# Ones column in v, PSUM scratch for half A's conversion, thresholds on ScalarE, reordered first loads, turns in half B

## The chip, the cores and the metric

One core of one Trainium2 chip. The metric is the device time of one execution in microseconds (us), lower is better.

## What is computed

Attention with a threshold on 4 batches of 8 heads, 576 positions of 64 numbers, and behind it two dense layers with gates on 2304 tokens (512 to 2048 to 512 each). All data are float32.

```python
scores = scale * np.matmul(q, k.transpose(0, 1, 3, 2))
thresh = np.max(scores, axis=-1, keepdims=True) - tau
scores = np.where(scores >= thresh, scores, -1000000000.0)
attn = np.exp(scores - np.max(scores, axis=-1, keepdims=True))
attn = attn / (np.sum(attn, axis=-1, keepdims=True) + 1e-09)
x = heads_to_columns(np.matmul(attn, v))          # [2304, 512]
h = x @ w1_in;  x = (h * np.clip(h + 3, 0, 6) / 6) @ w1_out
h = x @ w2_in;  return (h - np.tanh(h)) @ w2_out
```

## The kernel before

Every product is made from operands that are split in a high and a low part, three matmuls for one (`mm3`), so most tensors exist twice. The weights come as float32 and are converted on the chip.

**Who orders the work.** The kernel records tasks with `add(engine, duration, key, ...)`, and `Plan.issue` (L90) lays them out when the program is built: it plays the engines forward in time with the given durations, and whenever an engine is free it issues the task with the smallest key among those whose inputs are ready. The order on each engine is fixed by that; on the chip each engine goes through its list in order and waits at semaphores. A key is a priority and no time. Rings of buffers (`Ring`) are part of it; rings with `free=True` choose their slot when the task is issued. `slack` holds back a task's successors, and a buffer's reuse, in the plan only.

**Attention.** A unit (`softmax`, L556) is one head and 128 queries, or the last 64 queries of two heads (`c == NC`); there are 144. TensorE makes the scores into one of two PSUM buffers `s` (L580), VectorE takes the negative maximum (L585), ScalarE the exponential (L587), VectorE computes the threshold from the maximum (L589, one column) and multiplies the exponentials by "score at least threshold" (L592), where an accumulator gives the sum of the weights. ScalarE rounds the result to 16 bits (L597), GpSimd subtracts for the low part (L601), a transposing DMA on the queue of SP turns it (L604), and TensorE multiplies it with v (L637, `weighted`), from where ScalarE copies it into `x` (L647). The sums get 1e-9 added, are multiplied with v's scale (L609) and inverted (L613, L618) on VectorE. `v_round` (L505) scales and splits v, `k_round` and `q_round` transpose and split k and q. `x_round` (L655) normalises a block of x on GpSimd (L670), transposes and splits it. LK, LQ, LV tell how many units ahead k, q and v are prepared.

**First layer, half A.** The hidden dimension of 2048 is cut in halves of 8 pieces of 128. Half A runs beside attention, in 8 groups of 256 or 320 tokens (`layer1`, L700), as soon as a group's x is there. It accumulates in two PSUM banks of the ring `R_m`. Its 16 weights (`load_w`, L330) are converted beside the first units: a load on SP's queue, ScalarE's absolute value into the SBUF scratch `wu` (L353), four steps on VectorE on 512 columns (L356, L358, L361, L364), ScalarE's copy (L370) and GpSimd's subtraction (L372).

**First layer, half B, and second layer.** After attention the memory of attention is freed and taken for a second set of weights ("b"; the first is "a"). Half B goes through 9 blocks of 256 tokens: for each of 8 pieces `hidden` (12 matmuls, gate) and a second product (12 matmuls) into four PSUM banks, of which a block takes two. The blocks come one after the other. Its in weights are converted into the buffers "a", its out weights into "b". The second layer has its blocks 0 and 1 taking turns by halves already; its weights of the first half go to "b" (in) and "a" (out), those of the second to "a" (in) and "b" (out).

## Time and profile before

| | |
|---|---|
| median of 3 runs | 1166.88 us (1164.44 to 1168.1) |
| profiled execution | 1166.68 us |
| its span, first to last instruction | 1164.8 us |
| TensorE busy, mean granted clock | 1074.1 us, 0.959 |
| VectorE busy | 743.8 us |
| ScalarE busy | 608.8 us |
| GpSimd busy | 426.7 us |

PE is TensorE, PEld its loading of weights, DVE is VectorE, ACT is ScalarE, POOL is GpSimd, SP only issues DMAs. Times of an engine are the union of its instructions in time. Instructions that follow each other on one engine can overlap a little. A granted clock of 1 is TensorE's full speed.

### The profile page before, as it was taken

What the parts mean: (1) busy time and instruction counts of PE and PEld (TensorE: products, weight loads), DVE (VectorE), ACT (ScalarE), POOL (GpSimd) and SP (SyncE); (2) the same over time, 40 slices, a digit from 0 to 9 for tenths busy, and PEclk for the clock granted to TensorE, in tenths of its full rate; (3) what the DMA queues carried; (4) which work ended last, traced back from release to release, by engine and by line L of the source; (5) the groups of instructions that cost most, each with busy time, mean ns of one, the idle gap of its engine ahead of it and who ended that gap; (6) DMA issues with size and microseconds to landing.
All of it is one profiled execution on the core that took longest, in us unless ns stands there. A gap on an engine that the chain in (4) does not pass through costs nothing.

```text
span 1164.8 us, 23412 instructions
## 1 busy us (share of the span) xinstructions
PE 1074.1 (92%) x9104; PEld 1001.5 (86%) x9104; DVE 743.8 (64%) x1651; ACT 608.8 (52%) x1214; POOL 426.7 (37%) x412
## 2 busy tenths in 40 slices
PE   5647699999999899889899999999999999999998
PEld 4546689998999799888799999977999999999997
DVE  6999978688878877667766664697333333333332
ACT  7656678688768876554444443454323323233222
POOL 3665767666756675562321120265200000000000
PEclk8567899999999999999899999999999999999999
DMA  7788677869977767788543332132000000000000
GB/s 198 161 171 184 132 151 178 185 136 197 159 168 148 166 128 152 167 225 271 173 130 91 91 93 55 55 115 67 19 19 19 1 19 19 1 19 18 1 19 19
DMA packets 257455, 125.79 MB, mean 108 GB/s; under 512 B 200256, under 2 KB 250944, under 8 KB 257344
## 3 DMA queue, kind: packets, MB, share of 16 engines
q1 hardware_dynamic: 247840, 114.85, 42.3%
q0 software_dynamic: 9504, 9.44, 3.5%
q8 instruction: 72, 1.18, 0.4%
q14 instruction: 39, 0.32, 0.1%
HBM read 62.92 MB, written 18.87 MB: 70 GB/s over the span
## 4 chain that ended last, share of the span: by engine, by line
PE 46%; POOL 2%; issue 2%; DVE 1%; ACT 0%; POOLq 0%; DVEq 0%; ACTq 0%
PE ya L382 23%; PE h L382 12%; PE m L382 11%; POOL g L697 1%; POOL bo L372 1%; DVE st L361 0%; POOL ai L372 0%; DVE st L364 0%; DVE wu L358 0%; DVE y L925 0%; ACT x L938 0%; DVE wu L356 0%; DVE wu L991 0%; DVE x L941 0%; ACT ai L370 0%
## 5 line engine op out<-in xcount | busy, mean ns | idle before, releaser
L601 POOL TENSOR_TENSOR pp<-e,pp 128x128 f16<-128x128 f32 (+3 forms) x160 | 190.4, 1211 | 111.8 <-ACT pp L597 69.4
L697 DVE TENSOR_TENSOR g<-t,g 128x256 fp32r<-128x256 f32 x184 | 94.5, 514 | 72.0 <-ACT g L694 42.6
L694 ACT ACTIVATE g<-t 128x256 fp32r<-128x256 f32 x216 | 90.0, 417 | 96.4 <-DVE t L895 70.4
L580 PE MATMUL s<-ks,q 128*128 128x288 f32 x512 | 105.4, 334 | 35.9 <-DVE e L592 33.7
L592 DVE SCALAR_TENSOR_TENSOR e<-s,z,e 128x576 f32<-128x576 f32 x144 | 116.1, 812 | 25.8 <-ACT e L587 24.5
L585 DVE TENSOR_REDUCE z<-s 128x1 f32<-128x576 f32 x144 | 107.3, 751 | 26.5 <-PE s L580 25.3
L382 PE MATMUL m<-xT,ai 128*128 128x256 f32 (+1 forms) x768 | 120.7, 303 | 3.0 <-DVE t L689 2.6
L382 PE MATMUL h<-x,ai 128*128 128x256 f32 x864 | 117.1, 286 | 5.1 <-ACT ai L370 2.7
L580 PEld LDWEIGHTS s<-ks,q 128*128 128x128 f32 x512 | 82.0, 210 | 44.1 <-DVE e L592 19.1
L382 PEld LDWEIGHTS h<-x,ai 128*128 128x128 f32 x864 | 112.4, 194 | 8.8 <-ACT ai L370 2.9
L382 PE MATMUL ya<-g,bo 128*128 128x256 f32 x864 | 115.4, 284 | 1.8 <-DVE g L697 1.8
L382 PE MATMUL m<-x,ai 128*128 128x256 f32 x864 | 115.3, 283 | 1.2 <-DVE t L689 1.1
L587 ACT ACTIVATE e<-s,z 128x576 f32<-128x576 f32 x144 | 105.1, 738 | 21.3 <-DVE z L585 14.1
L382 PE MATMUL ya<-ao,g 128*128 128x512 f32 x432 | 113.2, 395 | 2.7 <-POOL g L697 2.7
L382 PEld LDWEIGHTS m<-x,ai 128*128 128x128 f32 x864 | 110.8, 191 | 4.9 <-DVE t L689 1.7
L382 PE MATMUL ya<-bo,g 128*128 128x512 f32 x432 | 112.1, 394 | 1.6 <-POOL g L697 1.6
L382 PEld LDWEIGHTS ya<-g,bo 128*128 128x128 f32 x864 | 109.1, 193 | 2.4 <-DVE g L697 2.4
L382 PEld LDWEIGHTS m<-xT,ai 128*128 128x128 f32 x768 | 107.1, 192 | 4.7 <-DVE t L689 3.3
L637 PE MATMUL tp<-vt,pt 128*128 128x64 f16 (+1 forms) x2240 | 88.9, 202 | 14.4 <-DVE ks L478 4.7
L637 PEld LDWEIGHTS <-pt 128*128 128x128 f16 (+1 forms) x2240 | 80.4, 107 | 22.9 <-issue 15.4
L895 DVE TENSOR_TENSOR t<-h,t 128x256 f32<-128x256 f32 x72 | 30.5, 423 | 99.3 <-ACT t L893 99.3
L597 ACT ACTIVATE pp<-e 128x1152 f16<-128x1152 f32 (+1 forms) x80 | 85.2, 1065 | 13.0 <-DVE e L592 10.8
(94 smaller groups left out, 1846.1 us busy)
## 6 DMA issues: line engine op xcount, KB each, us to landing
st<-in_moe_w_in_dram SPq DMA_DIRECT2D x32, 512.0 KB, 3.9
st<-in_moe_w_out_dram SPq DMA_DIRECT2D x32, 512.0 KB, 4.0
x<-xs POOLq DMA_DIRECT2D x18, 512.0 KB, 5.8
xs<-xT SPq DMA_DIRECT2D x8, 640.0 KB, 4.2
y<-ys SPq DMA_DIRECT2D x9, 512.0 KB, 9.8
kr<-in_k_dram SPq DMA_DIRECT2D x16, 256.0 KB, 3.1
vr<-in_v_dram SPq DMA_DIRECT2D x16, 256.0 KB, 3.5
qr<-in_q_dram SPq DMA_DIRECT2D x64, 64.0 KB, 2.5
```

What stands on the lines that cost most here:

```text
L372: add("pool", t_pool(DM), key + 3 + 5 * step, lambda: nc.gpsimd.tensor_tensor(out=put(1), in0=raw(1).bitcast(F32), in1=put(0).bitcast(F32) ...
L382: nc.tensor.matmul(ps, l[a], r[b], start=first and t == 0 and i == 0, stop=last and t == 2 and i == n - 1,)
L580: nc.tensor.matmul(ps.t[:, half, 0:SH], l, ks[:, half * SH:(half + 1) * SH], start=i == 0, stop=i == len(ops) - 1,)
L585: add("dve", 0.67, key, lambda: nc.vector.tensor_reduce(out=z.t[:, 0:1], in_=s(), axis=AX.XY, op=ALU.max, negate=True), r=[ps], w=[z])
L587: exp = add("act", 0.63, key, lambda: nc.scalar.activation(out=ex(), in_=s(), func=ACTF.Exp, bias=z.t[:, 0:1]), r=[ps, z], w=[e])
L592: add("dve", 0.74, key, lambda: nc.vector.scalar_tensor_tensor(out=ex(), in0=s(), scalar=z.t[:, 1:2], in1=ex(), op0=ALU.is_ge, op1=ALU.mul ...
L597: high = add("act", t_act(w * S, sbuf=True), key, lambda: nc.scalar.activation(out=pp.t[:, 0:w, 0:S], in_=e.t[:, 0:w, :], func=ACTF.Copy), ...
L601: add("pool", t_pool(w * (src.stop - src.start)), key, lambda src=src, dst=dst: nc.gpsimd.tensor_tensor(out=pp.t[:, 0:w, dst], in0=e.t[:, ...
L637: nc.tensor.matmul(pv.t[0:m, w_ * D:(w_ + 1) * D], pt.t[:, n, blk, rows], vv, start=o == 0, stop=o == len(ops) - 1)
L694: hi = add("act", t_act(n, sbuf=True), key, lambda: nc.scalar.activation(out=gh(), in_=t(), func=ACTF.Copy), r=[bt], w=[bh])
L697: add(low, t_pool(n) if low == "pool" else t_dve(n), key, lambda: eng.tensor_tensor(out=gl(), in0=t(), in1=gh().bitcast(F32), op=ALU.subtr ...
L895: add("dve", t_dve(n), key, lambda: nc.vector.tensor_tensor(out=s_(), in0=p(), in1=s_(), op=ALU.subtract), r=[ps, t], w=[t])
```

## The change

Seven edits, and new durations in the plan.

1. v gets a 65th column: ones in the high part, zeros in the low part (written once by GpSimd; the four buffers of v are fixed now). The product with v gives the sum of the weights as its 65th column. The accumulator of L592, L609, L613, L618 and their buffers go. One `scalar_tensor_tensor` and one reciprocal on VectorE per block of x (`invert`) do their work; v's scales are kept per batch in `sv`. GpSimd's normalising reads x at steps of 65 and writes it packed.
2. The 16 conversions of half A use a bank of `R_m` in PSUM as scratch in place of `wu`. In every conversion the third step now writes to the scratch and the fourth reads it from there, so the loaded tile is written by the fourth step only.
3. In units 0 to 53 the threshold is computed by ScalarE (`Identity` with scale and bias), after the exponential; behind them by VectorE as before.
4. The first k load goes ahead of the k rows of the last 64 positions; the first q load is issued on ScalarE's queue. q is prepared 3 units ahead for 2, v 1 unit ahead for 3. The keys of half A's weights lie 0.8 steps apart, before 1.5.
5. Half B: blocks 0 and 1 take turns, piece by piece through the first four, then four of block 0 and four of block 1.
6. All of half B's weights go to "b"; the second layer's first half to "a" and its second to "b".
7. In the plan alone, groups of layer one and the hidden products of half B keep their order among themselves (`turn`), and the second products of half A come after all its out weights are converted.

```diff
-    LK, LQ, LV, LD = 5, 2, 3, 4
+    LK, LQ, LV, LD = 5, 3, 1, 4
...
-    W0, WS, WO = 8.0, 1.5, -2.0
+    W0, WS, WO = 8.0, 0.8, -2.0
...
+    ZU = 54
+    ST, SB, CS = 4.0, 2.0, 0.0
...
-    R_v = at_ring(at_p, NP, [128, 2, 2, NC + 1, D], F16, "vt")
-    R_vs = at_ring(at_p, NP + 2, [128, 3], F32, "vs")
+    vt_t = [at_p.tile([128, 2, 2, NC + 1, D + 1], F16, name=f"vt{j}") for j in range(NP)]
+    R_v = [Ring(1, lambda j=j: vt_t[j]) for j in range(NP)]
+    at_rings += R_v
+    R_vs = at_ring(at_p, 2, [128, 2], F32, "vs")
+    R_sv = at_ring(at_p, 2, [128, H], F32, "sv")
     R_q = at_ring(at_p, 2, [128, 2, 2, 256], F32R, "q")
     R_e = at_ring(at_p, 2, [128, 2, S], F32, "e")
     R_pp = at_ring(at_p, 2, [128, 2, 2 * S], F16, "pp")
     R_pt = at_ring(at_p, 2, [128, 2, 2 * NC + 1, 128], F16, "pt")
     R_z = at_ring(at_p, 8, [128, 2], F32, "z")
-    R_rs = at_ring(at_p, 8, [128, 4], F32, "rs")
-    R_x = at_ring(at_p, 2, [128, 2, DM], F32, "x")
-    R_xl = at_ring(at_p, 1, [128, 1, DM], F32, "xl")
-    R_rx = at_ring(at_p, 3, [128, 2, H], F32, "rx")
-    R_rl = at_ring(at_p, 2, [128, 1, H], F32, "rl")
+    R_x = at_ring(at_p, 2, [128, 2, H, D + 1], F32, "x")
+    R_xl = at_ring(at_p, 1, [128, 1, H, D + 1], F32, "xl")
+    R_rx = at_ring(at_p, 2, [128, 2, H], F32, "rx")
+    R_rl = at_ring(at_p, 1, [128, 1, H], F32, "rl")
...
-    R_m = ring(ps_m, 2, [128, 512], F32, "m")
+    R_m = Ring(2, lambda i: ps_m.tile([128, 512], F32, tag=f"m{i}", name="m"), free=True)
...
-    def load_w(name, kind, m, src, half, key, step, after=(), slack=0.0):
-        wst, wu, W = R_st.new(), R_wu.new(), R_w[name, kind, m].new()
+    def load_w(name, kind, m, src, half, key, step, after=(), slack=0.0, scratch=None, cs=0.0):
+        wst, wu, W = R_st.new(), (scratch or R_wu).new(), R_w[name, kind, m].new()
...
-                out=raw(1), in0=raw(1), scalar=-0x40000000, in1=part(I32),
+                out=part(I32), in0=raw(1), scalar=-0x40000000, in1=part(I32),
                 op0=ALU.bitwise_and, op1=ALU.bitwise_or),
             lambda: nc.vector.scalar_tensor_tensor(
-                out=raw(1).bitcast(U32), in0=raw(0).bitcast(U32), scalar=29, in1=raw(1).bitcast(U32),
+                out=raw(1).bitcast(U32), in0=raw(0).bitcast(U32), scalar=29, in1=part(U32),
                 op0=ALU.logical_shift_right, op1=ALU.bitwise_or),
         ]
         for n, f in enumerate(steps):
-            add("dve", 0.8 if n > 1 else 0.5, key + 3 + n * step, f, r=[[wu], [wu], [wu, wst], [wst]][n], w=[wu] if n < 2 else [wst])
+            add("dve", 0.65 if n > 1 or scratch else 0.5, key + 3 + n * step, f,
+                r=[wu] if n < 2 else [wu, wst], w=[wu] if n < 3 else [wst], slack=cs)
...
+        queue = nc.sync if eng == "dma" else nc.scalar
         for i in range(2):
-            add("dma", 0.47, key, lambda i=i: nc.sync.dma_start(
+            add(eng, 0.47, key, lambda i=i: queue.dma_start(
...
+        part = lambda i: vt.t[:, i, :, :, 0:D].rearrange("p h c d -> p (h c) d")
...
+            nc.vector.reciprocal(out=sv.t[:, 2 * j:2 * j + 2], in_=vs.t[:, 1:2].to_broadcast([128, 2]))
...
-        add("dve", 0.13, key, lambda: nc.vector.tensor_scalar(
-            out=z.t[:, 1:2], in0=z.t[:, 0:1], scalar1=-1.0, scalar2=tau_b[:, 1:2],
-            op0=ALU.mult, op1=ALU.subtract), r=[z], w=[z])
+        if u < ZU:
+            add("act", 0.2, key, lambda: nc.scalar.activation(
+                out=z.t[:, 1:2], in_=z.t[:, 0:1], func=ACTF.Identity, scale=-1.0, bias=tau_b[:, 3:4]), r=[z], w=[z], after=[exp])
+        else:
+            add("dve", 0.15, key, lambda: nc.vector.tensor_scalar(
+                out=z.t[:, 1:2], in0=z.t[:, 0:1], scalar1=-1.0, scalar2=tau_b[:, 1:2],
+                op0=ALU.mult, op1=ALU.subtract), r=[z], w=[z])
         add("dve", 0.74, key, lambda: nc.vector.scalar_tensor_tensor(
-            out=ex(), in0=s(), scalar=z.t[:, 1:2], in1=ex(), op0=ALU.is_ge, op1=ALU.mult,
-            accum_out=rs.t[:, i:i + 1]), r=[ps, e, z], w=[e, rs])
+            out=ex(), in0=s(), scalar=z.t[:, 1:2], in1=ex(), op0=ALU.is_ge, op1=ALU.mult),
+            r=[ps, e, z], w=[e])
...
-        if u == ui[-1]:
-            wi = len(ui)
-            add("dve", 0.25, key, lambda: nc.vector.tensor_scalar(
-                out=rs.t[:, 0:wi], in0=rs.t[:, 0:wi], scalar1=1e-9, scalar2=vs.t[:, 2:3], op0=ALU.add, op1=ALU.mult),
-                r=[rs, vs], w=[rs])
-            if wi > 1:
-                add("dve", 0.095, key, lambda: nc.vector.reciprocal(
-                    out=rx.t[:, :, 2 * j:2 * j + 2].rearrange("p c h -> p h c"),
-                    in_=rs.t[:, 0:wi].rearrange("p (h c) -> p h c", c=2)), r=[rs], w=[rx])
-            else:
-                for x in range(2):
-                    add("dve", 0.075, key, lambda x=x: nc.vector.reciprocal(
-                        out=rx.t[0:LF, 0, 2 * j + x:2 * j + x + 1], in_=rs.t[x * LF:(x + 1) * LF, 0:1]), r=[rs], w=[rx])
...
-                        pv.t[0:m, w_ * D:(w_ + 1) * D], pt.t[:, n, blk, rows], vv, start=o == 0, stop=o == len(ops) - 1)
+                        pv.t[0:m, w_ * (D + 1):(w_ + 1) * (D + 1)], pt.t[:, n, blk, rows], vv, start=o == 0, stop=o == len(ops) - 1)
...
+        if c == 0 and i != 1:
+            rx = RX[xi] = R_rx.new() if i == 0 else R_rl.new()
+            cs, sv = 2 if i == 0 else 1, SV[b]
+
+            def invert():
+                nc.vector.scalar_tensor_tensor(
+                    out=rx.t[0:w], in0=xt.t[0:w, :, :, D], scalar=1e-9,
+                    in1=sv.t[0:w].unsqueeze(1).to_broadcast([w, cs, H]), op0=ALU.add, op1=ALU.mult)
+                nc.vector.reciprocal(out=rx.t[0:w], in_=rx.t[0:w])
+
+            add("dve", 0.4, key - 7.5, invert, r=[xt, sv], w=[rx])
+        rx = RX[xi]
...
-                out=x, in0=x, in1=rx.t[0:w, c, :].unsqueeze(2).to_broadcast([w, H, D]), op=ALU.mult)
+                out=xn().rearrange("p (h d) -> p h d", h=H), in0=xt.t[0:w, c, :, 0:D],
+                in1=rx.t[0:w, c, :].unsqueeze(2).to_broadcast([w, H, D]), op=ALU.mult)
...
-            prev = []
+            prev = turn[-1:]
...
-            prev = []
+            prev = [x for m in range(MH) for x in W["o", m].writers]
...
+        for t in vt_t:
+            for i in range(2):
+                nc.gpsimd.memset(t[:, i, :, :, D:D + 1].rearrange("p h c d -> p (h c) d"), 1.0 - i)
...
+                    load_k(b, j, key - LD * STEP)
                     if j == 0:
                         load_k_left(b, key - LD * STEP)
-                    load_k(b, j, key - LD * STEP)
...
+                load_q(b, g, j, key - LD * STEP, "act" if (b, g, j) == (0, 0, 0) else "dma")
...
+                    "a", kind, m, w1_in if kind == "i" else w1_out, 0, T0 + STEP * (W0 + WS * n + WO * (kind == "o")), 0.8, slack=ST, scratch=R_m, cs=CS)
...
-        WB = weights(1, {"i": "a", "o": "b"}, w1_in, w1_out, start - FW + WBO, WBS, lambda n: late)
+        WB = weights(1, {"i": "b", "o": "b"}, w1_in, w1_out, start - FW + WBO, WBS, lambda n: late)
...
+        steps, xb, accs, before = [], {}, {}, {}
+        if len(blocks) > 1:
+            work = [(x, m) for m in range(MH // 2) for x in (0, 1)]
+            work += [(x, m) for x in (0, 1) for m in range(MH // 2, MH)]
+        else:
+            work = [(0, m) for m in range(MH)]
+        work += [(i, m) for i in range(2, len(blocks)) for m in range(MH)]
+        for i, m in work:
+            c, n = blocks[i]
+            if m == 0:
+                xb[i] = load_x(c, n, key - XL2)
+                accs[i] = [R_ya.new() for _ in range(KD // 2)]
+            acc = accs[i]
...
+            steps.append(add(
+                "pe", t_mm(n, 3 * KD), key + 2.1 * PM * 2, second, r=[WB["o", m], g], w=acc, after=before.get(i, ())))
+            before[i] = steps[-1:]
...
-            weights(0, {"i": "b", "o": "a"}, w2_in, w2_out, T2, (key - T2) / 16, lambda n: [steps[(n * (len(steps) - 16)) // 16]]),
-            weights(1, {"i": "a", "o": "b"}, w2_in, w2_out, key - W2B, W2S, lambda n: [steps[-6]]),
+            weights(0, {"i": "a", "o": "a"}, w2_in, w2_out, T2, (key - T2) / 16, lambda n: [steps[(n * (len(steps) - 16)) // 16]]),
+            weights(1, {"i": "b", "o": "b"}, w2_in, w2_out, key - W2B, W2S, lambda n: [steps[-6]]),
```

## Rows read from the trace of the kernel before

**Rows 1.** The page: its first line, the span.

```profile
span 1164.8 us, 23412 instructions
```

**Rows 2.** Table by stretches: busy time (x instructions) per engine, then clock, DMA share, GB/s.

```profile
core 0: us, PE busy (x) PEld busy (x) DVE busy (x) ACT busy (x) POOL busy (x), PEclk, DMA share, GB/s
0.00:30.00 30.00, 17.61 (x72) 13.73 (x72) 19.22 (x54) 21.89 (x38) 10.00 (x16) 0.84 0.79 196
30.00:150.00 120.00, 76.95 (x763) 69.03 (x764) 111.72 (x234) 78.06 (x136) 77.61 (x68) 0.68 0.75 158
150.00:480.00 330.00, 320.03 (x3620) 303.53 (x3619) 266.65 (x692) 256.12 (x478) 216.93 (x219) 0.99 0.80 164
480.00:570.00 90.00, 74.47 (x592) 70.66 (x591) 60.69 (x99) 41.74 (x84) 42.14 (x36) 0.96 0.75 219
570.00:740.00 170.00, 170.00 (x1419) 170.00 (x1418) 101.60 (x199) 70.31 (x151) 28.93 (x27) 1.00 0.32 90
```

**Rows 3.** Groups of VectorE, first 150 us: count | busy us, mean ns | idle before.

```profile
L364 DVE SCALAR_TENSOR_TENSOR st<-st 128x512 uint32<-128x512 uint32 x16 | 16.7, 1042 | 0.0
L361 DVE SCALAR_TENSOR_TENSOR st<-st,wu 128x512 int32<-128x512 int32 x16 | 15.8, 985 | 0.0
L356 DVE TENSOR_SCALAR wu<-wu 128x512 f32<-128x512 f32 x16 | 10.8, 678 | 1.0 <-ACT wu L353 1.0
L358 DVE TENSOR_SCALAR wu<-wu 128x512 int32<-128x512 int32 x16 | 10.0, 622 | 0.1
...
L589 DVE TENSOR_SCALAR z<-z,tau_b 128x1 f32<-128x1 f32 x35 | 6.7, 204 | 0.1
L609 DVE TENSOR_SCALAR rs<-rs,vs 128x4 f32<-128x4 f32 (+1 forms) x10 | 4.4, 439 | 0.0
...
L592 DVE DVE_READ_ACCUMULATOR e<-s,z,e 128x1 f32 x35 | 2.8, 80 | 0.0
...
L613 DVE RECIPROCAL rx<-rs 128x4 f32<-128x4 f32 x7 | 1.2, 167 | 0.0
L618 DVE RECIPROCAL rl<-rs 64x1 f32<-64x1 f32 x6 | 0.9, 152 | 0.0
```

**Rows 4.** Timeline of the first stage: start us, duration us, what [idle before].

```profile
46.43 3.00 POOL L601 TENSOR_TENSOR pp<-e,pp 128x128 f16<-128x128 f32 x2 [1.32 <-issue]
...
47.70 2.01 DVE L356 TENSOR_SCALAR wu<-wu 128x512 f32<-128x512 f32 x1
...
91.48 0.41 DVE L356 TENSOR_SCALAR wu<-wu 128x512 f32<-128x512 f32 x1
...
93.56 0.68 DVE L361 SCALAR_TENSOR_TENSOR st<-st,wu 128x512 int32<-128x512 int32 x1
```

**Rows 5.** Groups of the whole run: the copy of 512 columns from PSUM.

```profile
L991 DVE COPY wu<-ya 128x512 f32<-128x512 f32 x18 | 11.6, 682 | 1.6 <-PE ya L382 1.6
```

**Rows 6.** Groups of ScalarE, first 150 us.

```profile
L647 ACT ACTIVATE x<-tp 128x128 f32<-128x128 f32 x14 | 3.9, 276 | 11.5 <-PE tp L637 11.5
...
L515 ACT ACTIVATION_READ_ACCUMULATOR vt<-vr 128x1 f32 x6 | 1.1, 190 | 0.0
```

**Rows 7.** Waits of TensorE, 10 to 150 us: in total, times, longest.

```profile
PE s L580 <- DVE e L592: 30.3, 16, 5.9
```

**Rows 8.** Timeline: the first scores.

```profile
12.05 2.59 PE L580 MATMUL s<-ks,q 128*128 128x288 f32 x8 [0.32 <-ACT q L483]
```

**Rows 9.** Timeline of TensorE at full clock: the product of two units with v.

```profile
307.16 0.99 PE L637 MATMUL tp<-vt,pt 128*128 128x64 f16 x28
```

**Rows 10.** Timeline, half B's first and last weight on GpSimd; the chain, one run in half B.

```profile
494.09 1.32 POOL L372 TENSOR_TENSOR bo<-st,bo 128x512 fp32r<-128x512 f32 x1
...
562.90 1.48 POOL L372 TENSOR_TENSOR bo<-st,bo 128x512 fp32r<-128x512 f32 x1
...
582.44 1.44 PE m L382 x12
```

More of the change, by code (lines that the diff above doesn't have):

```diff
@@ L57, in slot_at @@
     def slot_at(self, now):
-        return min((x, i) for i, x in enumerate(self.slots))[1] if min(self.slots) <= now else None
+        return min((x, i) for i, x in enumerate(self.slots))[1] if min(self.slots) <= now + 1e-6 else None
 class Plan:
@@ L147, in issue @@
                 for b in t.free:
-                    b.ends.append(end + self.LAT[t.eng])
+                    b.ends.append(end + self.LAT["dma" if t.xfer else t.eng])
                     if len(b.ends) == len(b.users):
@@ L353, in load_w @@
         add("act", t_act(DM, sbuf=True), key + 3, lambda: nc.scalar.activation(
-            out=part(F32), in_=raw(1).bitcast(F32), func=ACTF.Abs), r=[wst], w=[wu])
+            out=part(F32), in_=raw(1).bitcast(F32), func=ACTF.Abs), r=[wst], w=[wu], slack=cs)
         steps = [
@@ L404, in attention_moe_moe_kernel @@
     NU = len(units)
-    KR, QR, VR, KL, QL, KS, VT, VS, QT = ({} for _ in range(9))
+    KR, QR, VR, KL, QL, KS, VT, SV, QT = ({} for _ in range(9))
     def load_k_left(b, key):
@@ L445, in load_q @@
         copy = lambda r: t.t[:, :, :, r, :].rearrange("p h c d -> p (h c) d")
-        add("pool", 0.68, key + 4, lambda: nc.gpsimd.tensor_copy(copy(1), copy(0)), r=[t], w=[t])
+        add("pool", 0.5, key + 4, lambda: nc.gpsimd.tensor_copy(copy(1), copy(0)), r=[t], w=[t])
     def transposes(ps, srcs):
@@ L549, in sum_group @@
         return [x for x in (u - 1, u, u + 1) if 0 <= x < NU and units[x][:4] == (b, g, j, h)]
-    def inv_group(u):
-        b, g, j, h, c = units[u]
-        return [x for x in range(max(u - 3, 0), min(u + 4, NU)) if units[x][:3] == (b, g, j) and (units[x][3] is None) == (h is None)]
     def softmax(u, key):
@@ L625, in weighted @@
         us, vt, pv = sum_group(u), VT[b, j], R_tp.new()
-        xt = XT[b, g if h is not None else "l"][0]
+        xi = (b, g if h is not None else "l")
+        if xi not in XT:
+            XT[xi] = R_x.new() if h is not None else R_xl.new()
+        xt = XT[xi]
         work = [(slice(0, 128), h % 2, n) for n in range(len(us))] if h is not None else [
@@ L733, in layer1 @@
                         r=[W["o", m], r[m]], w=[ps], after=prev)]
+                    if p == 0 and m == 0:
+                        last = prev[0]
             second.append(prev[0])
@@ L739, in layer1 @@
                 out=part(), in_=y.t[:, 0:n]), r=[y], xfer=0.4))
+        turn.append(last)
         return first, second
@@ L904, in attention_moe_moe_kernel @@
             load_y(i, T2 - YL + i)
-        steps = []
-        for i, (c, n) in enumerate(blocks):
-            x = load_x(c, n, key - XL2)
-            acc = [R_ya.new() for _ in range(KD // 2)]
-            into = lambda d, acc=acc, n=n: acc[d // 2].t[:, d % 2 * n:(d % 2 + 1) * n]
-            for m in range(MH):
-                g = hidden(WB, m, x, n, 1, key)
-                def second(m=m, g=g, into=into, n=n):
-                    for d in range(KD):
-                        s = slice(d * 128, (d + 1) * 128)
-                        w = WB["o", m].t
-                        mm3(into(d), [((w[:, 0, s], w[:, 1, s]), (g.t[:, 0, 0:n], g.t[:, 1, 0:n]))],
-                            first=m == 0 and d % 2 == 0, last=m == MH - 1 and d % 2 == 1)
-                steps.append(add(
-                    "pe", t_mm(n, 3 * KD), key + 2.1 * PM * 2, second, r=[WB["o", m], g], w=acc, after=steps[-1:]))
-                key += 2 * PM
-            for h in range(KD // 2):
-                add("dve", t_dve(2 * n), key + 2 * PM, lambda h=h, i=i, acc=acc, n=n: nc.vector.tensor_tensor(
-                    out=Y[i].t[:, 2 * h:2 * h + 2, :], in0=acc[h].t[:, 0:2 * n].rearrange("p (d n) -> p d n", d=2),
-                    in1=Y[i].t[:, 2 * h:2 * h + 2, :], op=ALU.add), r=[acc[h], Y[i]], w=[Y[i]])
@@ new lines, in attention_moe_moe_kernel, with second @@
+        steps, xb, accs, before = [], {}, {}, {}
[11 more added lines that the diff above has]
+            acc = accs[i]
+            g = hidden(WB, m, xb[i], n, 1, key)
+            def second(m=m, g=g, acc=acc, n=n):
+                for d in range(KD):
+                    s = slice(d * 128, (d + 1) * 128)
+                    w = WB["o", m].t
+                    mm3(acc[d // 2].t[:, d % 2 * n:(d % 2 + 1) * n],
+                        [((w[:, 0, s], w[:, 1, s]), (g.t[:, 0, 0:n], g.t[:, 1, 0:n]))],
+                        first=m == 0 and d % 2 == 0, last=m == MH - 1 and d % 2 == 1)
+            steps.append(add(
+                "pe", t_mm(n, 3 * KD), key + 2.1 * PM * 2, second, r=[WB["o", m], g], w=acc, after=before.get(i, ())))
+            before[i] = steps[-1:]
+            key += 2 * PM
+            if m == MH - 1:
+                for h in range(KD // 2):
+                    add("dve", t_dve(2 * n), key + 2 * PM, lambda h=h, i=i, acc=acc, n=n: nc.vector.tensor_tensor(
+                        out=Y[i].t[:, 2 * h:2 * h + 2, :], in0=acc[h].t[:, 0:2 * n].rearrange("p (d n) -> p d n", d=2),
+                        in1=Y[i].t[:, 2 * h:2 * h + 2, :], op=ALU.add), r=[acc[h], Y[i]], w=[Y[i]])
```

71 lines of the change are left out of this document (30 added, 41 removed).

## The prediction

> **What bounds the kernel now.** I read the page first, then the table by stretches, then VectorE's groups in the first 150 us, the timeline there, and last the turn from half A to half B. The profiled execution took 1166.68 us, 1.88 us more than its span [rows 1]; the median of the three runs is 1166.88 us, so a sum made against the profile holds for the median within 0.2 us. About 0.3% (3.5 us) is what a measurement of this kernel can tell from no change.
>
> The table shows two stages with slack [rows 2]. In the first 150 us TensorE is busy for 17.6 + 77.0 = 94.6 us, and that at a granted clock of 0.84 and 0.68, so partly at the lower of its two levels of 1.2 and 2.4 GHz. VectorE is busy for 111.7 of the 120 us from 30 to 150, 93%: it is the bound of that stage. With the first 30 us it has 130.9 us, ScalarE 21.9 + 78.1 = 100.0 us. The longest wait of TensorE says the same: scores wait 30.3 us for VectorE's masking step to free their PSUM buffer [rows 7]. The other stage is 480 to 570 us, where TensorE idles 90 - 74.5 = 15.5 us and the clock is 0.96. From 570 to 740 us TensorE has no gap, and the second layer behind that is not touched in order or amount; I leave both as they are.
>
> Two things fill VectorE in the first stage besides the softmax itself [rows 3]. The conversion of half A's 16 weights takes 16.7 + 15.8 + 10.8 + 10.0 = 53.3 us. The small operations (threshold, accumulator read, sums, reciprocals) take 6.7 + 2.8 + 4.4 + 1.2 + 0.9 = 16.0 us. Many of these are not slow by themselves: L356 takes 0.41 us in one place and 2.01 us in another, where GpSimd is in a 3.00 us subtraction that it began before; L361 takes 0.68 us undisturbed [rows 4] and 0.985 us in the mean of the stage.
>
> **The change part by part.**
>
> *Ones column.* It removes the accumulator reads (35 in the stage, 2.8 us) and L609, L613, L618 (6.5 us) [rows 3]. These are durations; neighbouring instructions of VectorE overlap a little, so I count the second part between 4.6 and 6.5 us. It adds two instructions (add-and-scale, reciprocal) per block of x, three such pairs in the stage; by L609 and L613 a pair costs 0.44 + 0.17 = 0.6 us, 1.8 us in all. Net 5.6 to 7.5 us; I take 6.5. The pair now lies between the last copy of x and GpSimd's normalising, so the end of each group gets 0.6 us longer; other work covers this but at the last group, where nothing else is left: 0.6 us once, inside my figure for the turn. In TensorE 2240 matmuls get 65 columns for 64. 28 of them take 0.99 us at full clock [rows 9], 35 ns each at most; one column in 64 more is 0.55 ns each, 1.2 us at most over the run. Eight small memsets on GpSimd stand at its start, where it has no work yet; uncovered, at 0.4 us each (as much as the smallest VectorE step on 512 columns), they would cost 3 us.
>
> *Thresholds on ScalarE.* All 35 units of the stage lie below 54. VectorE loses 6.7 us of durations, about 4 us if overlap is taken off; I take 5. ScalarE gains 35 instructions on one column. No row shows this one; the nearest are its accumulator read on one column, 0.19 us, and its copy of 128 columns, 0.276 us [rows 6]: 6.7 to 9.7 us, and I take 7, since one column is the nearer shape. ScalarE then has 107 us in the stage. The threshold stands behind the exponential in ScalarE's queue, and the next unit's exponential and the copies behind it; VectorE's masking waits for it 0.2 us longer. With two score buffers and a unit each 150/35 = 4.3 us this is covered as long as ScalarE isn't the bound (a rival below).
>
> *PSUM scratch.* Each of the four VectorE steps of a weight now has an operand in PSUM. Undisturbed they take 0.41 + 0.41 + 0.68 + 0.68 = 2.18 us (the second and fourth taken as the first and third); a copy of 512 columns out of PSUM takes 0.682 us [rows 5], so four steps take 2.73 us, 43.6 us for 16 weights, against the 53.3 us measured: 9.7 us less, provided that steps fed from PSUM are not held while GpSimd works. Bounds: 53.3 - 34.9 = 18 us less, if PSUM cost nothing extra and all waiting went; 8.8 us more, if the waiting stays and the slower rate comes on top. The rows speak for the first proviso, as the long cases lie where GpSimd is at work [rows 4]. A rule of the Trainium skill speaks against this part: VectorE: DVE Perf Modes, section "Why PSUM operands drop a tier", says that an operand in PSUM holds an fp32 instruction to its lowest rate, since PSUM has one read port for VectorE where SBUF has two. The rows agree on the rate (0.41 against 0.682 us); by that rule alone the change of place would lose 8.8 us.
> The two banks are those in which layer one accumulates, so layer one's first group can wait for a conversion to end. The weights' keys now lie 0.8 steps apart instead of 1.5, so the conversions should be through before that group starts; if not, the group ends later by what is left of them.
>
> *First loads.* The first scores start at 12.05 us [rows 8]. Now k's main part goes first, q goes by ScalarE's queue, and the first v conversion comes later. This gives up to 3 us, or nothing if ScalarE's two issues delay its first copies of k; I take 2.
>
> *Sum of the first stage.* 6.5 + 5 + 9.7 = 21 us of VectorE's 131 us go; by the bounds 1 to 31. What is late next is ScalarE at 107 us, nearly level with VectorE's 110. Two engines that feed each other at the same load keep less than the 93% of one alone, so I take 17 of the 21, and with the first loads 19 us.
>
> *150 to 480 us.* TensorE is busy for 320 of 330 us. VectorE loses some 25 us more here that nobody waits for. I take 3 us for fewer waits of TensorE; bounds 8 less and 5 more (the extra column, and the rule that groups of layer one keep their turn).
>
> *Half B.* GpSimd begins the last step of the first of its 16 weights at 494 us and of the last at 563 us [rows 10]: 4.6 us per weight, 9.2 us per pair of in and out weight, where one block gives TensorE two runs of 1.44 us, 2.88 us, per pair. Two blocks in turn give 5.76 us, so much of the waiting for weights is covered: of the 15.5 us idle and some 3 us of low clock I take 7 back. What stays is the end of attention before 494 us, where nothing else can run, and the last pair, ready only at 564 us whatever the order. Bounds 0 and 13. Half B's first weights now go to buffers that open when attention has ended, and 494 us is when attention ends, so nothing there.
>
> Sum: 1166.7 - 19 - 3 - 7 = 1137.7, so **1138 us**.
>
> **The rivals.**
> *ScalarE takes over.* With 107 us and the threshold behind the exponential in each unit it becomes the bound, and the first stage gives only 8 us: 1166.7 - 8 - 3 - 7 = 1149. For it: the loads are nearly level. Against: ScalarE is busy for 78 of 120 us now, 65%. Chance 0.18.
> *More than forecast.* VectorE keeps its density: 21 us less of work at 93% is 23 us, with 3 for the start 26; with 8 in the middle and 13 in the turn 1166.7 - 47 = 1120. Against: three upper ends at once. Chance 0.13.
> *The waiting stays.* The blocked time isn't tied to operands in SBUF and stays, and the slower PSUM rate is added: VectorE's 21 us become 21 - 9.7 - 8.8 = 2.5, so 1166.7 - 2.5 - 3 - 7 = 1154. Against it: the overlap with GpSimd [rows 4]. The page named above gives the slower rate here too. Chance 0.08.
> *Slower.* v's rows begin 130 bytes apart instead of 128. If TensorE reads such rows slower, each of 2240 matmuls pays, most of them in the stage where it is the bound. The 29 us gained are gone at 29/2240 = 13 ns per matmul, over a third of their 35 ns; at double the duration it is 78 us, 1216. Nothing in the trace shows such a read. Chance 0.07.
>
> **How the numbers follow.** Forecast 0.52, its own range 1128 to 1148; the rivals 0.18, 0.13, 0.08 and 0.07; 0.02 for others. The range holds the forecast, ScalarE's case and most of the two beside them: 1117 to 1155. Faster by over 0.3% (below 1163): 0.88; within 0.3%: 0.04; slower: 0.08.
>
> **What would show it.** Right, if the conversion steps take about 0.68 us each with no 2 us among them in the first 150 us, VectorE needs some 110 us for the same 35 units and 16 weights, layer one's first group ends some 20 us earlier, 28 products with v still take 0.99 us, and TensorE idles below 10 us in the 90 us around the turn. Wrong, if ScalarE is busy for over 90% of the first stage, if the products with v lengthen, or if layer one waits for its PSUM banks.

## The result and the profile after

The median of the kernel after is 1146.4 us (1145.7 to 1148.5, 4 runs) against 1166.6 us before: a ratio of 0.983, with a 95% interval of 0.981 to 0.985. That is 20 us less where 29 were forecast, and inside the forecast's own range of 1128 to 1148. The profiled execution took 1146.78 us, with a span of 1144.7 us.

The table by stretches of the kernel after (busy time and instructions of PE, PEld, DVE, ACT, POOL; granted clock, DMA share, GB/s) answers to [rows 2]:

```profile
0.00:30.00 30.00, 16.12 (x65) 12.70 (x65) 18.89 (x40) 21.37 (x38) 10.29 (x24) 0.80 0.72 186
30.00:150.00 120.00, 92.29 (x949) 82.39 (x950) 105.48 (x176) 93.32 (x192) 80.12 (x76) 0.78 0.85 181
150.00:480.00 330.00, 317.53 (x3589) 301.66 (x3589) 251.94 (x491) 254.76 (x489) 213.88 (x217) 0.99 0.79 163
480.00:570.00 90.00, 83.88 (x623) 82.08 (x622) 70.78 (x121) 47.06 (x93) 40.20 (x35) 0.97 0.80 234
```

From 30 to 150 us TensorE is busy for 15 us more, and at a higher granted clock (0.78 for 0.68). VectorE is still the busiest, at 105 of 120 us, and ScalarE at 93 us is not full. Around the turn TensorE idles 6.1 us where it idled 15.5.

The groups of the first 150 us of the kernel after (count | busy us, mean ns | idle before) answer to [rows 3]. L361 to L369 are the four conversion steps, L660 and L663 the new pair per block of x, L587 the threshold on ScalarE:

```profile
L361 DVE TENSOR_SCALAR m<-m 128x512 f32<-128x512 f32 x16 | 11.0, 690 | 2.6 <-ACT m L358 2.6
L363 DVE TENSOR_SCALAR m<-m 128x512 int32<-128x512 int32 x16 | 11.0, 689 | 0.0
L366 DVE SCALAR_TENSOR_TENSOR m<-st,m 128x512 int32<-128x512 int32 x16 | 11.0, 685 | 0.0
L369 DVE SCALAR_TENSOR_TENSOR st<-st,m 128x512 uint32<-128x512 uint32 x16 | 10.8, 673 | 0.0
...
L660 DVE SCALAR_TENSOR_TENSOR rx<-x,sv 128x16 f32<-128x16 f32 x2 | 2.2, 1124 | 1.2 <-ACT x L635 1.1
...
L663 DVE RECIPROCAL rx<-rx 128x16 f32<-128x16 f32 x2 | 0.5, 254 | 0.1
```

```profile
L587 ACT ACTIVATE z<-z,tau_b 128x1 f32<-128x1 f32 x39 | 10.9, 290 | 0.0
```

The conversions take 11.0 + 11.0 + 11.0 + 10.8 = 43.8 us. The forecast was 43.6 us, and all four steps have one duration now: none is held, the longest of the 64 takes 0.70 us. The threshold takes 0.29 us where 0.2 was taken, above the upper bound of 0.276 [rows 6].

Waits of TensorE from 10 to 150 us (total, times, longest), and two lines of its timeline (start, duration): the first scores, and a product of two units with v. They answer to [rows 7 to 9].

```profile
PE s L577 <- DVE e L593: 18.7, 14, 4.9
```

```profile
10.36 1.31 PE L577 MATMUL s<-ks,q 128*128 128x288 f32 x4
...
183.50 1.03 PE L628 MATMUL tp<-vt,pt 128*128 128x65 f16 x28
```

The scores' wait for the masking step falls from 30.3 to 18.7 us, the first scores start 1.7 us earlier, and 28 products with 65 columns take 1.03 us for 0.99.

To see where the 20 us lie, both runs are cut at the same events: the end of the scores of the 36th unit (the last of the first batch), the end of layer one's first group, the last scores, the end of half A, the end of half B. First the kernel before, then after:

```profile
0.00:151.47 151.47, 96.02 (x846) 84.23 (x847) 132.29 (x290) 101.29 (x175) 88.45 (x84) 0.72 0.75 165
151.47:169.10 17.63, 17.44 (x205) 16.83 (x204) 14.22 (x39) 12.84 (x24) 10.26 (x10) 1.00 0.76 178
169.10:473.70 304.60, 294.82 (x3336) 279.10 (x3335) 247.40 (x641) 238.21 (x446) 200.57 (x205) 0.99 0.79 161
473.70:528.05 54.35, 46.88 (x419) 44.98 (x419) 34.28 (x56) 26.11 (x53) 33.15 (x29) 1.00 0.78 204
528.05:749.50 221.45, 213.38 (x1742) 211.30 (x1742) 139.75 (x267) 95.41 (x200) 45.63 (x40) 0.98 0.40 118
```

```profile
0.00:132.20 132.20, 91.02 (x775) 78.26 (x776) 112.65 (x197) 104.00 (x207) 78.02 (x89) 0.76 0.85 188
132.20:154.25 22.05, 21.65 (x275) 20.85 (x274) 15.57 (x26) 14.80 (x33) 15.20 (x15) 0.96 0.73 146
154.25:460.00 305.75, 296.32 (x3346) 281.68 (x3343) 234.88 (x461) 241.62 (x462) 200.14 (x204) 0.99 0.80 162
460.00:514.30 54.30, 47.26 (x397) 45.46 (x396) 36.93 (x55) 25.67 (x52) 32.33 (x29) 0.94 0.75 199
514.30:728.00 213.70, 211.58 (x1755) 210.57 (x1754) 142.05 (x269) 95.75 (x200) 45.81 (x41) 1.00 0.42 121
```

The lengths differ by -19.27, +4.42, +1.15, -0.05 and -7.75 us; the second layer behind them takes 1.4 us more. Together -20.1 us.

### The profile page after: what moved, and what is told of

Same layout as the page of the kernel before. It is cut to its first block, busy times and chain, and to the rows that moved or that the text cites. A ratio compares the mean times of both kernels' runs of the same rounds, so it can differ in the third digit from the quotient of the medians.

```text
span 1144.7 us, 23228 instructions
## 1 busy us (share of the span) xinstructions
PE 1073.2 (94%) x9104; PEld 1002.1 (88%) x9104; DVE 718.4 (63%) x1365; ACT 616.5 (54%) x1268; POOL 419.0 (37%) x420
## 4 chain that ended last, share of the span: by engine, by line
PE 74%; DVE 8%; issue 5%; ACT 5%; POOL 3%; DMA 3%; SPq 0%; POOLq 0%; DVEq 0%; ACTq 0%
PE ya L388 24%; PE m L388 18%; PE h L388 12%; PE s L577 7%; PE m L734 6%; PE tp L628 5%; DVE e L593 2%; PE tp L460 2%; POOL bi L378 1%; DVE z L582 1%; ACT e L584 1%; POOL g L701 1%; DMA pt<-pp 1%; DMA st<-in_moe_w_in_dram 1%; DVE st L369 1%
## 5 line engine op out<-in xcount | busy, mean ns | idle before, releaser
L602 POOL TENSOR_TENSOR pp<-e,pp 128x128 f16<-128x128 f32 (+3 forms) x160 | 185.4, 1179 | 119.3 <-ACT pp L598 58.3
L593 DVE SCALAR_TENSOR_TENSOR e<-s,z,e 128x576 f32<-128x576 f32 x144 | 116.1, 811 | 15.6 <-ACT e L584 9.9
L577 PE MATMUL s<-ks,q 128*128 128x288 f32 x512 | 105.2, 334 | 17.2 <-DVE e L593 16.5
L388 PE MATMUL h<-x,bi 128*128 128x256 f32 x864 | 115.4, 283 | 0.1
L388 PE MATMUL m<-x,bi 128*128 128x256 f32 x864 | 115.1, 283 | 0.0
L388 PEld LDWEIGHTS h<-x,bi 128*128 128x128 f32 x864 | 111.0, 191 | 3.3 <-POOL bi L378 0.3
L388 PEld LDWEIGHTS m<-x,bi 128*128 128x128 f32 x864 | 111.0, 191 | 3.0
L628 PE MATMUL tp<-vt,pt 128*128 128x65 f16 (+1 forms) x2240 | 87.9, 199 | 8.1 <-DMA pt<-pp 4.5
L388 PEld LDWEIGHTS ya<-ao,g 128*128 128x128 f32 x432 | 75.9, 189 | 21.1 <-POOL g L701 7.8
```

The lines of the kernel that those rows point to most:

```text
L388: nc.tensor.matmul(ps, l[a], r[b], start=first and t == 0 and i == 0, stop=last and t == 2 and i == n - 1,)
L577: nc.tensor.matmul(ps.t[:, half, 0:SH], l, ks[:, half * SH:(half + 1) * SH], start=i == 0, stop=i == len(ops) - 1,)
L593: add("dve", 0.74, key, lambda: nc.vector.scalar_tensor_tensor(out=ex(), in0=s(), scalar=z.t[:, 1:2], in1=ex(), op0=ALU.is_ge, op1=ALU.mul ...
L602: add("pool", t_pool(w * (src.stop - src.start)), key, lambda src=src, dst=dst: nc.gpsimd.tensor_tensor(out=pp.t[:, 0:w, dst], in0=e.t[:, ...
L628: nc.tensor.matmul(pv.t[0:m, w_ * (D + 1):(w_ + 1) * (D + 1)], pt.t[:, n, blk, rows], vv, start=o == 0, stop=o == len(ops) - 1)
```

## The experiments

The whole change gains 20 us. Undoing one of four parts (the scratch, the thresholds, the loads with the lookahead, the turns) costs 11 to 35 us, so the parts don't add up, and four later runs (the plan's durations, the scratch with durations as measured, the lookahead alone, 36 units) ask why. The ones column has no run of its own, so its share is not shown. The median of the kernel before in these jobs was 1166.8 to 1167.1 us.

**Scratch back in SBUF.** `, scratch=R_m, cs=CS)` becomes `, cs=CS)` in the loads of half A.

> The changed kernel with one part undone: half A's 16 conversions use the SBUF scratch again. Theory (GpSimd holds back VectorE steps whose operands all lie in SBUF): the four steps of a weight go back to a mean near 3.3 us in the first 150 us, with single ones of 1 to 2.5 us, VectorE gets about 9 us more work there, and the time rises by 6 to 9 us, to 1152 to 1155 us. Rival (the waiting does not hang on the operands' place, PSUM only gives the slower rate): the steps take 2.2 us per weight when undisturbed and the time falls or stays, 1140 to 1146 us.

Measured: 1181.3 us (1178.8 to 1183.6), slower than the kernel before (ratio 1.012, 1.010 to 1.014). Its groups of VectorE in the first 150 us, and its timeline around 44, 64 and 73 us, GpSimd first:

```profile
L369 DVE SCALAR_TENSOR_TENSOR st<-st,wu 128x512 uint32<-128x512 uint32 x15 | 17.8, 1185 | 0.0
L366 DVE SCALAR_TENSOR_TENSOR wu<-st,wu 128x512 int32<-128x512 int32 x15 | 16.3, 1087 | 0.1
L361 DVE TENSOR_SCALAR wu<-wu 128x512 f32<-128x512 f32 x15 | 13.8, 922 | 3.0 <-ACT wu L358 2.8
L363 DVE TENSOR_SCALAR wu<-wu 128x512 int32<-128x512 int32 x15 | 8.3, 555 | 0.0
```

```profile
43.18 2.51 POOL L602 TENSOR_TENSOR pp<-e,pp 128x128 f16<-128x128 f32 x2 [2.61 <-issue]
...
63.40 2.51 POOL L602 TENSOR_TENSOR pp<-e,pp 128x128 f16<-128x128 f32 x2 [2.34 <-issue]
...
72.82 1.30 POOL L378 TENSOR_TENSOR ai<-st,ai 128x512 fp32r<-128x512 f32 x1 [4.12 <-ACT ai L376]
```

```profile
43.95 2.03 DVE L361 TENSOR_SCALAR wu<-wu 128x512 f32<-128x512 f32 x1
...
64.23 2.23 DVE L369 SCALAR_TENSOR_TENSOR st<-st,wu 128x512 uint32<-128x512 uint32 x1
...
73.01 1.66 DVE L366 SCALAR_TENSOR_TENSOR wu<-st,wu 128x512 int32<-128x512 int32 x1
```

The step of 64.23 us ends at 66.46, 0.55 us after GpSimd's ended at 65.91; that of 73.01 us ends at 74.67, 0.55 us after GpSimd's 74.12. Undisturbed they take 0.68 us. All 13 steps of these two lines above 1 us in the first 150 us end 0.54 to 0.55 us after an instruction of GpSimd. So a step with both operands in SBUF does not run slower beside GpSimd; it stands until GpSimd is through and then does nearly all of its work. The Trainium skill says this in SBUF — State Buffer, "Who interferes with whom": an instruction of VectorE with two SBUF inputs contends with a GpSimd instruction that reads SBUF, and the ports that they share are an exclusive lock. The trace agrees, with 2.23 and 1.66 us for 0.68. Here the steps with one operand, in SBUF too, stand in the same way: eight of L361 and L363 take 0.98 to 2.07 us for 0.41, and each ends 0.28 or 0.29 us after GpSimd, as the one at 43.95 us. The conversions take 3.75 us per weight here, 60.0 us for 16, against 43.8: 16 us more of VectorE, and the scores' wait for the masking step rises to 42.1 us. That is no more than half of the 35 us lost, where 6 to 9 us were expected.

**All thresholds on VectorE, all on ScalarE.** `ZU = 54` becomes 0 in one run and 144 in the other.

> The changed kernel with one part undone: all thresholds on VectorE. Theory of the forecast (VectorE bounds the first stage, ScalarE has room): 35 to 40 thresholds of 0.2 us come back to VectorE there and the time rises by 3 to 6 us, to 1149 to 1152 us. Rival (after the other parts VectorE is no longer the bound, and the threshold behind the exponential, 0.29 us on ScalarE where 0.2 was forecast, only lengthens each unit's chain): no loss or a gain, 1141 to 1146 us.

> The changed kernel with all 144 thresholds on ScalarE. Theory (where TensorE is full neither engine's small work is waited for): no change within 2 us of 1146 us. Rival (the threshold on ScalarE, behind the exponential, lengthens the chain from scores to weights in each unit, and scores wait for their buffer longer): 1149 to 1155 us, with more waiting of the scores on the masking step between 150 and 460 us than the 5.3 us of the changed kernel.

Measured: 1162.5 us (1162.3 to 1163.7) and 1159.2 us (1158.3 to 1159.8). Both lose far more than was expected. With 0 the 36th unit's scores end at 143.7 us for 132.2, but those of the 40th only 5.0 us later than in the kernel after, those of the 57th 9.8 and the last 16.1 us later. Behind the 54th unit no threshold has moved, so the 6.3 us that are lost behind the 57th are lost with the same work. With 144 no unit's scores up to the 49th are over 1.2 us off, and the loss lies in the middle, where ScalarE is busy for 81% only (from 154.8 us to the last scores at 473.4; the kernel after takes 305.75 us for that stretch):

```profile
154.80:473.42 318.62, 300.24 (x3378) 284.47 (x3376) 226.77 (x372) 258.01 (x552) 202.00 (x204) 0.99 0.77 158
```

The longer chain of the rival shows there: VectorE's masking waits 17.1 us for the threshold of ScalarE (0.7 us in the kernel after), and the scores wait 9.1 us for the masking, for 5.3. That is less than the 13 us lost; the rest stays open.

**No turns in half B.** The blocks 0 and 1 go one after the other.

```diff
-            work = [(x, m) for m in range(MH // 2) for x in (0, 1)]
-            work += [(x, m) for x in (0, 1) for m in range(MH // 2, MH)]
+            work = [(x, m) for x in (0, 1) for m in range(MH)]
```

> The changed kernel with one part undone: half B's blocks come one after the other, with all else kept, the buffers of half B too. Theory (block 0 alone cannot fill TensorE while the weights of half B arrive): TensorE's idle time between the end of half A and the end of half B rises by 7 to 8 us and the time by as much, to 1153 to 1155 us; the end of attention stays at 475 us. Rival (the gain of that stretch came from the other buffers or from an earlier start of the conversions): the time stays within 2 us of 1146 us.

Measured: 1157.8 us (1156.9 to 1158.7), 11.4 us lost where 7 to 8 were expected. Half A ends at 513.3 us, 1 us from the kernel after; all of it is half B, at 224.80 us for 213.70:

```profile
513.30:738.10 224.80, 214.97 (x1755) 213.77 (x1754) 142.59 (x269) 95.40 (x200) 45.37 (x41) 0.97 0.40 115
```

**The turns alone**, put into the kernel before with its old buffers for half B.

> The kernel before with one part of the change alone: blocks 0 and 1 of half B take turns, with the old buffers (in weights of half B in the first set). Theory: the stretch from the end of half A to the end of half B shortens by 6 to 8 us and the time falls to 1159 to 1161 us; what comes before is untouched. Rival (the new buffers are needed for it, since in the old ones the last group's products must be over before a weight can land): a gain below 3 us, 1164 to 1167 us.

Measured: 1160.0 us (1158.4 to 1162.8), 6.8 us won. Half B takes 214.10 us for 221.45:

```profile
527.20:741.30 214.10, 210.37 (x1730) 209.16 (x1730) 139.05 (x266) 94.29 (x198) 44.97 (x40) 0.99 0.43 122
```

With and without the rest of the change the turns are worth 7 to 11 us, in the place where they stand, and with the old buffers too. The other runs bear this out, if the stretch is taken from the last scores on, since half A's end is no clean mark (in the kernel before, half B's first products begin at 506.6 us, ahead of it). From the last scores to the end of half B all eleven kernels with turns take 267.6 to 270.6 us, the three without 273.2 (the scratch alone, below, where the stretch from half A's end takes 214.95 us, no more than with turns), 275.8 (the kernel before) and 278.9 us (no turns). So the turns stand out from the scatter of the other edits, but their size is known to some us only.

**The PSUM scratch alone**, put into the kernel before, with the third step's result in the scratch.

> The kernel before with one part of the change alone: PSUM scratch for half A's conversions, and in all conversions the third step's result in the scratch. Theory (VectorE steps with one operand in PSUM are not held back by GpSimd): four steps take 2.7 us per weight in place of 3.3, VectorE saves near 10 us of the first 150 us, and the time falls by 6 to 10 us, to 1157 to 1161 us. Rival (the slower rate comes on top of the waiting): the time rises by up to 8 us, to 1167 to 1175 us.

Measured: 1162.2 us (1160.3 to 1162.9), 4.7 us won. VectorE's four steps take 11.1, 11.1, 11.1 and 11.0 us in the first 150 us, 9 us less than before. The scores of the 36th unit end 10.5 us earlier, those of the 40th 5.3 and the last 6.4 us earlier. The part that costs 35 us when it is undone gains 5 when it is done alone, a little less than the 6 to 10 us expected.

**First loads and lookahead.** One run puts back the old order of the first loads and `LQ, LV = 2, 3` for 3, 1; another the lookahead alone.

> The changed kernel with one part undone: first loads in the old order, first q on SP's queue, q and v prepared 2 and 3 units ahead as before. Theory (the first scores start 1.7 us earlier and VectorE was the bound): the first scores come 1.5 to 2 us later and the time rises by 1 to 3 us, to 1147 to 1149 us. Rival (the earlier start is lost again before TensorE is full, or the late v rounds cost as much as the early q rounds bring): within 1 us of 1146 us, or below.

> The kernel after with q prepared 2 units ahead and v 3 units ahead, as before, and the new order of the first loads kept. It splits the run e5, which put both back and took 1158.8 us. If the loads carry e5's loss: 1146 to 1149 us. If the lookahead carries it: 1155 to 1158 us; the v conversions then stand two units earlier on ScalarE and VectorE in the first stage. If it is the order dealt anew, the two parts don't add up to 12 us: anything else.

Measured: 1158.8 us (1157.0 to 1161.1) and 1158.6 us (1156.1 to 1160.6), the first 10 us above its theory. The new order of the loads starts the scores at 10.40 us for 12.05 in these two runs, and the time does not follow. By the times alone the lookahead would carry it all, but the two runs lose in different places. Against the kernel after, the 16th unit's scores end 12.4 us later with the lookahead alone, and 1.9 us earlier with both parts undone. In the latter run the 37th unit's are still within 0.7 us, and the 40th's are 7.4 us late. So two orders came to the same time in different ways, and what either part is worth by itself is not shown.

**The order of layer one's groups.** `prev = turn[-1:]` becomes `prev = []` in the first products.

> The changed kernel without the rule that a group of layer one begins behind its predecessor's last products. It tells where 5 us went that were gained by unit 35 (20 us ahead) and not there at the end of attention (14 to 16 us ahead). Theory (the rule opens gaps between the groups): the end of attention comes 3 to 5 us earlier than 475 us and the time falls to 1141 to 1144 us. Rival (the loss is layer one's products that had not been made by unit 35, and products with 65 columns, 1 to 1.4 ns more each): no change within 2 us of 1146 us.

Measured: 1147.6 us (1145.4 to 1149.8): no change. The rule is not what cost the middle its gain.

**The plan's durations.** No instruction changes, only two numbers by which the plan lays out the order.

```diff
-            add("act", 0.2, key, lambda: nc.scalar.activation(
+            add("act", 0.29, key, lambda: nc.scalar.activation(
...
-            add("dve", 0.4, key - 7.5, invert, r=[xt, sv], w=[rx])
+            add("dve", 1.25, key - 7.5, invert, r=[xt, sv], w=[rx])
```

> The kernel after, with two durations in the plan set to what its trace shows: ScalarE's threshold 0.29 us for 0.2, the reciprocal pair of x 1.25 us for 0.4. No instruction is added or removed; only the planned order on the engines can differ. Theory 'the order is dealt anew by any edit of the first stage, and that alone moves the time by several us': a time that differs from 1146.4 us by 4 us or more in either direction, with the same counts of instructions. Rival 'the excess of the undo runs is the work that they put back': 1146 within 3 us, since no work changes; perhaps 2 us faster from truer durations.

Measured: 1162.9 us (1161.1 to 1165.0, 10 runs), 16.5 us lost with the same work. The 36th unit's scores end at 144.5 us for 132.2, layer one's first group 9.7 us later than in the kernel after, the last scores 13.7 us and the end of half B 15.7 us later, so most of the loss lies in the first stage. TensorE's wait for the masking step is back at 30.6 us:

```profile
PE s L577 <- DVE e L593: 30.6, 16, 4.2
```

The scores of the 28th unit still end 1.7 us earlier than in the kernel after (100.8 for 102.5 us), those of the 31st 11.6 us later (123.7 for 112.1). The timeline shows what lies between: VectorE of this run, and then of the kernel after in the same part of the stage.

```profile
107.47 0.81 DVE L593 SCALAR_TENSOR_TENSOR e<-s,z,e 128x576 f32<-128x576 f32 x1
...
112.40 0.42 DVE L693 SCALAR_TENSOR_TENSOR t<-t,m 128x256 f32<-128x256 f32 x1 [2.06 <-ACT t L691]
...
117.17 0.42 DVE L693 SCALAR_TENSOR_TENSOR t<-t,m 128x256 f32<-128x256 f32 x1 [0.71 <-ACT t L691]
...
120.01 0.42 DVE L693 SCALAR_TENSOR_TENSOR t<-t,m 128x256 f32<-128x256 f32 x1 [2.10 <-ACT t L691]
121.21 0.82 DVE L593 SCALAR_TENSOR_TENSOR e<-s,z,e 128x576 f32<-128x576 f32 x1 [0.77 <-ACT z L587]
```

```profile
108.88 0.41 DVE L693 SCALAR_TENSOR_TENSOR t<-t,m 128x256 f32<-128x256 f32 x1
...
109.83 0.82 DVE L593 SCALAR_TENSOR_TENSOR e<-s,z,e 128x576 f32<-128x576 f32 x1
...
112.42 0.41 DVE L693 SCALAR_TENSOR_TENSOR t<-t,m 128x256 f32<-128x256 f32 x1
...
114.71 0.82 DVE L593 SCALAR_TENSOR_TENSOR e<-s,z,e 128x576 f32<-128x576 f32 x1
```

L693 is a step of layer one's gate, L593 the masking. With the new numbers VectorE stands 2.06, 0.71 and 2.10 us for a gate whose input from ScalarE isn't there, and no masking step runs between 108.3 and 121.2 us. In the kernel after the gates find their input ready, and masking steps lie between them. TensorE's granted clock differs there too. First this run, then the kernel after:

```profile
100.00:122.00 22.00, 19.03 (x184) 17.59 (x183) 15.80 (x27) 13.86 (x33) 10.00 (x10) 0.74 0.81 182
```

```profile
100.00:122.00 22.00, 19.68 (x210) 18.03 (x210) 21.63 (x40) 20.03 (x48) 16.49 (x18) 1.00 0.91 199
```

TensorE was busy for only 5.4 us of the 10 before this stretch, for 9.4 in the kernel after, and then makes 184 products in 19.0 us where the other makes 210 in 19.7. So the new order costs waits and clock together; how much each is was not settled.

**The SBUF scratch with durations as measured.** As the first run, with 0.92, 0.56, 1.09 and 1.19 us in the plan for the four steps.

> The kernel after with the scratch of half A's conversions back in SBUF, as in the run e1, but with the four steps' durations in the plan at what e1's trace shows (0.92, 0.56, 1.09, 1.19 us for 0.5, 0.5, 0.65, 0.65). Theory 'e1 lost its 35 us to work, 16 us of VectorE's steps that are held beside GpSimd, and to the waits behind them': 1175 to 1183 us, as e1. Rival 'half of it was a plan that took these steps for 1.5 us shorter per weight than they are': 1158 to 1168 us, and the waits of the scores for the masking step back from 42 us to about 25 us in the first 150 us.

Measured: 1171.3 us (1170.1 to 1173.7, 10 runs), between the two expectations: with truer durations in the plan 10 us of the 35 are gone, and the scores' wait falls from 42.1 to 26.7 us. This order is a newly laid one as well, so the 10 us are not the price of the durations alone. The steps' means, 0.66, 0.63, 1.38 and 0.98 us, still come to 58.3 us for 16 weights, 14.5 more than in PSUM. So 25 us remain against the kernel after, beside 14.5 us more of VectorE's work; how the time divides between this work, waits behind it and again the order is open.

**36 units on ScalarE.** `ZU = 54` becomes 36.

> The kernel after with ScalarE's thresholds in units 0 to 35 for 0 to 53. The work of the first 130 us is the same, 18 thresholds of the middle go back to VectorE, which has slack there. By work alone 1145 to 1148 us. If the order dealt anew is what the runs with 0 and 144 units mostly show, it moves by 4 us or more although no engine that is short of time gets more work.

Measured: 1147.1 us (1146.6 to 1148.2): the same. Up to the 36th unit, at 131.8 us, it goes as the kernel after, and 18 thresholds in the middle are worth nothing that shows.

## Why the prediction was right, and where its steps were off

*The sign and the place were right.* The time went in the first stage and in half B, as put. Of the 9 us that are missing from the 29, 4 were lost in the first stage, 4 in the middle and 1.4 in the second layer, which I had left as it was; the turns gave 0.75 more.

*PSUM scratch: right, as VectorE's work in size too.* 43.8 us for 43.6. What it gives in time apart from the rest is shown only by the run with the scratch alone, 4.7 us in an order of its own. The proviso (steps fed from PSUM are not held) holds: 16 of each step at 0.67 to 0.69 us on average. The blocked time was tied to operands in SBUF, as the run with the scratch back shows. The rule of the Trainium skill that spoke against the part (VectorE: DVE Perf Modes, "Why PSUM operands drop a tier") holds as well, at 0.69 us for the 0.41 of an undisturbed step [rows 4]; it is simply the smaller of the two. The rival in which the waiting stays falls.

*Thresholds: mis-sized.* I took 0.2 us, with bounds of 0.19 and 0.276; it takes 0.29. The nearer row in shape, a read of an accumulator, was not the nearer in kind. The Trainium skill has this number: ScalarE: Activation LUTs, "What ACT_TABLE_LOAD costs", gives 280 ns plus 0.833 ns per column for an instruction whose bias is a pointer, as it is here. The trace agrees, 290 ns for one column. ScalarE was not the bound with it: it has 104.0 us in the 132.2 us to the 36th unit, 79%, against 85% of VectorE. The rival in which ScalarE takes over gave a time near the one measured, 1149 us, but not by its mechanism.

*The pair per block of x: mis-sized, and harmless.* I took 0.6 us; in the first 150 us it took 1.12 + 0.25 us. Both its operands lie in SBUF, and the one at 145.87 us took 1.71 us and ended at 147.58, 0.03 us after a step of GpSimd; the other took 0.54. Two pairs in the stage: 1.6 us more than put.

*First loads: nothing that shows, where I took 2 us.* The scores do start 1.7 us earlier, and the first unit's end 2.0 us earlier, but the fourth's end 1.0 us later than before.

*VectorE's sum: right, the 19 us from it in part by luck.* It has 112.65 us up to the 36th unit, where it had 132.29: 19.6 us less, forecast 21. (The upper bound of 31 should be 32, as the thresholds' own upper value is 6.7; nothing hangs on it.) Scores of that unit end 19.3 us earlier, forecast 19. But I had 17 of the 21 for VectorE and 2 for the loads; VectorE's 19.6 us came nearly whole, and the 2 do not show. And this unit lies near a peak: from the 40th unit on the lead is 11 to 17 us, 13.7 at the last.

*What is late next: this step failed.* I named ScalarE. It was TensorE with layer one's first group. At the 36th unit's scores the kernel before had done 476 products with v and 14 of the second products (L730); the kernel after has done 420 and none of its L734. Groups of TensorE up to that event, before and after:

```profile
L637 PE MATMUL tp<-vt,pt 128*128 128x64 f16 (+1 forms) x476 | 25.1, 227 | 11.1 <-DVE qs L485 4.0 <-DVE xT L677 2.3 <-DVE ks L478 2.2
...
L730 PE MATMUL m<-gh,ao 128*128 128x256 f32 x14 | 3.3, 365 | 0.0
```

```profile
L628 PE MATMUL tp<-vt,pt 128*128 128x65 f16 (+1 forms) x420 | 20.6, 219 | 3.7 <-DMA pt<-pp 2.6 <-DVE vs L531 0.5 <-DVE q L492 0.4
```

TensorE then runs almost without a gap (21.65 of 22.05 us), and layer one's first group ends 14.9 us earlier, not 19. The idle time of this stage had been used by the second stream, too; the stage shrank by what both had gained.

*The middle: wrong sign.* I took 3 us less; it takes 1.2 us more (305.75 for 304.60 us). The 65th column is one reason that the trace shows: 1.03 for 0.99 us is 1.4 ns per product, where I allowed 0.55: 2.6 us over the 1792 products of this form, 1288 of them here (the others, of the last 64 positions, take 1.07 us per 28 before and after). The price for a read of rows 130 bytes apart that the last rival needs, 13 ns, is not there. VectorE's 12.5 us less in the middle (234.88 for 247.40) gave nothing that shows. I had said so, and took 3 us all the same.

*The turns: right.* 7.75 us for 7, and 7.4 and 11.1 us in the two runs that have them alone or lack them alone.

*The signs of being wrong.* Two of the three showed, both small: the products with v lengthen (1.03 for 0.99 us), and layer one waits 0.7 us in all for a bank that a conversion holds. ScalarE stays at 93.3 of 120 us, 78%.

*A term that the sum lacked.* It priced the work of each part and held the order for given. The run with two durations changed in the plan has the same work and takes 16.5 us more, nearly the whole gain. So the gain of 20 us is that of this work in this order, and parts that were undone one by one (the thresholds with 0 and 144, the lookahead) show their work and a newly laid order in one number. How they divide was not settled: the order can't be held while the work changes. The range of 38 us covered such a term by chance, not by reasoning.

## What to carry to other kernels

Where a greedy plan lays out the order, run the unchanged work once with slightly different durations before pricing single parts: that scatter (16.5 us of 1146 in the one such run here) has to be set against every comparison of one part. Beside a busy GpSimd, count for each step of VectorE how many operands lie in SBUF; one operand moved to PSUM costs at most 0.28 us per 512 columns here, and saves waits of up to 1.7 us (2.34 us for 0.68 in the run with the scratch back). When the bound of a stage is relieved, compare the amount of every stream's work at the same event, or the gain is read too high.
